# Two matrix-vector products of batch 1 on TensorE instead of VectorE, in a decode layer with its gradients

## The chip, the core and the metric

The kernel runs on one core of a Trainium2 chip. The core has a matrix engine (TensorE, PE in the profile), three engines for elementwise work (VectorE or DVE, ScalarE or ACT, GpSimd or POOL), a queue engine (SyncE or SP), 16 DMA engines, an on-chip memory SBUF of 128 partitions and an accumulator memory PSUM of eight banks. The metric is the device time of one execution in microseconds. Differences of about one per cent are at the edge of what can be told apart here.

## The reference

The layer is one decode step of attention over a cache, followed by a two-layer perceptron with ReLU, both with a layer norm ahead and a residual. Wanted are the output and the gradients with respect to seven of the inputs:

```python
h  = x + attention(layernorm(x), k_cache, v_cache, wq) @ wo
h2 = h + relu(layernorm(h) @ w1) @ w2
_out, _vjp = jax.vjp(_f, A_x, A_k_cache, A_v_cache, A_wq, A_wo, B_w1, B_w2)
```

(The first two lines are the reference's in short.) There are B = 2 batches with one token each, D = 640, H = 32 heads of 128, a cache of 4096 positions per head, and a hidden width Dff = 1728. Everything is bf16. K and V caches are 64 tiles of 1 MB each, and their gradients (out_2, out_3) are as large, so nearly all of the 363 MB moved are cache tiles.

Two small products of the backward pass are the subject here, both a weight matrix times a gradient vector of one batch:

- gx2 = w1 x ghf: 640 results, each a sum over 1728 (ghf is the gradient at the hidden layer, masked by ReLU);
- go = wo x gh1: 32 heads x 128 results, each a sum over 640 (gh1 is the gradient at h).

## The kernel before

The work is a list of *turns*, written out by hand as generators that are stepped against each other. The first sweep (`p1_iter`) visits the 64 pairs of batch and head: it loads K and V (1 MB each), transposes K in groups of blocks on TensorE (L405; ACT copies the result from PSUM, L410), forms scores, softmax and the products with V. The second sweep (`p2_iter`) visits the pairs again. In each of its turns TensorE transposes V in four groups of four f32 blocks (L426, copied by ACT at L431), takes products with go (L439) into `dp`, VectorE forms `gsp` (L823) and the two gradients gK and gV in halves of 128 x 2048 elements (L810), and POOL's queue stores them (L848, L867). V is loaded once more for it (tile `Wt`, L447, SP's queue), except for a few heads whose tile was kept. The two sweeps overlap for a while; from about 510 us on the second runs alone.

Between them lies the perceptron of each batch, `middle_gen`, a background generator. Its steps are dealt out by credit: at every step of the sweep `bg_step` adds a rate (0.8 in the part that matters here) and runs background steps until their own prices, the numbers they yield, have used it up. For batch 1 it runs beside turns 13 and following of the second sweep.

There the two products are made on VectorE. The gradient vector lies in columns, so `bcast_cols` (L619) spreads it first to a row on all partitions: TensorE multiplies broadcast columns by the identity into PSUM, and ACT copies the row to SBUF (tiles `fbc` and `hbc`). Then `ttr` (L640) multiplies a stretch of the natural weight tile with the row and sums along it: for w1 15 calls of 576 elements (five chunks of D, three thirds of Dff), for wo 32 calls of 640 elements, one a head. Each call waits for a `turn()` (L647): the main loop hands out one such slot in three of a turn's steps (L1154).

When a group of heads is summed, the rest of `go_group` (L665 to L686) rounds it, makes the paired form `gom` that the second sweep needs, and the products with MT that give the query's gradient `GQc`; it then marks the heads as done. The groups of batch 1 are heads 27 to 31, then eight at a time from 0.

What follows depends on it. After the mark ("w1", 1) the w1 tile is given up and `fin_gen` starts: the outer products of the weight gradients (`outer_rows`, L895), which use the PSUM banks of the list "o" in rotation, are copied to SBUF by ACT (L923), or one in three by VectorE (L921) once all heads are done, and stored from ACT's queue. After the last head `gx_gen` starts: it transposes wq on TensorE (L981), with ACT copying (L983), and takes products (L991), one group behind the transposes. `mlp_out` follows the heads in `middle_gen`. The transposes of all of these share two PSUM banks (role "tps") and five SBUF buffers (tag XT).

Of the kernel before, what the change touches and what calls it, by code (L numbers as in the profile page):

```python
# [7 lines left out]
FP32 = mybir.dt.float32  # L8
# [7 lines left out]
def kernel(  # L16
# [638 lines left out]

    def go_group(b, h0, h1, hbc):

        hs = slice(h0, h1)
        n = h1 - h0
        go32 = small.tile([128, GH], FP32, tag="go32", bufs=1, name="go32")  # L660
        for k in range(n):
            yield from turn()
            ttr(wo_t[:, h0 + k, :], hbc[:], go32[:, k:k + 1], D)
            yield 0.9
        nc.vector.tensor_copy(out=goc[:, hs, b], in_=go32[:, 0:n])  # L665
        pr = small.tile([128, GH], FP32, tag="pr", bufs=1, name="pr")
        nc.vector.tensor_tensor(out=pr[:, 0:n], in0=goc[:, hs, b], in1=OU[:, b, hs], op=ALU.mult)
        yield from wait(2)
        pair_rows(gom, goc, hs, slice(b, b + 1))
        yield from wait(2)  # L670
        d_ps = pst([128, 2, GH], FP32, "mid", "d_ps")
        nc.tensor.matmul(d_ps[:, 0, 0:n], lhsT=ones_f32, rhs=pr[:, 0:n], start=True, stop=True)
        for k in range(n):
            h = h0 + k
            nc.tensor.matmul(d_ps[:, 1, k:k + 1], lhsT=MTs.pop((b, h))[:], rhs=goc[:, h, b:b + 1],
                             start=True, stop=True)
        nc.vector.tensor_scalar(out=negdot[:, hs, b], in0=d_ps[:, 0, 0:n], scalar1=-1.0, scalar2=None, op0=ALU.mult)
        ud = small.tile([128, GH], FP32, tag="ud", bufs=1, name="ud")
        nc.vector.tensor_tensor(out=ud[:, 0:n], in0=Uc[:, b, hs], in1=negdot[:, hs, b], op=ALU.mult)
        mg = small.tile([128, GH], FP32, tag="mg", bufs=1, name="mg")  # L680
        nc.vector.tensor_tensor(out=mg[:, 0:n], in0=d_ps[:, 1, 0:n], in1=rt[:, b, hs], op=ALU.mult)
        nc.vector.tensor_tensor(out=ud[:, 0:n], in0=mg[:, 0:n], in1=ud[:, 0:n], op=ALU.add)
        nc.vector.tensor_scalar(out=GQc[:, hs, b], in0=ud[:, 0:n], scalar1=SCALE, scalar2=None, op0=ALU.mult)
        for h in range(h0, h1):
            done.add(("go", b, h))
        yield  # L686

    def mlp_out():

        ml32 = small.tile([128, ND, B], FP32, tag="ml32", bufs=1, name="ml32")  # L690
        nc.vector.memset(ml32[:], 0.0)
        for k in range(NW2):
            while free["q"] < 1:
                yield
            t = load_w2(k, "q", "(p c) d -> p c d")
            yield from wait(12)
            c1 = min(NF, (k + 1) * FP)
            m_ps = pst([128, ND, B], FP32, "mid", "mlp_ps")
            for c in range(ND):
                for cf in range(k * FP, c1):  # L700
                    kc = f_kc(cf)
                    nc.tensor.matmul(m_ps[:, c, :], lhsT=t[0:kc, cf - k * FP, c * 128:(c + 1) * 128],
                                     rhs=arow[0:kc, cf, :], start=(cf == k * FP), stop=(cf == c1 - 1))
            give(t)
            yield
            nc.vector.tensor_tensor(out=ml32[:], in0=m_ps[:], in1=ml32[:], op=ALU.add)
        ml_bf = small.tile([128, ND, B], BF16, tag="ml_bf", bufs=1, name="ml_bf")
        nc.vector.tensor_copy(out=ml_bf[:], in_=ml32[:])
        y_bf = small.tile([128, B, ND], BF16, tag="y_bf", bufs=1, name="y_bf")
        nc.vector.tensor_tensor(out=y_bf[:].rearrange("p b c -> p c b"), in0=h1c[:], in1=ml_bf[:], op=ALU.add)  # L710
        yield from wait(3)
        for b in range(B):
            store_row(y_bf[:, b, :], ND, out_0[b].rearrange("s (c p) -> (s c) p", p=128))
            yield

    def middle_gen(b):
        while a_next[0] < (b + 1) * H // OG:
            if o_next[0] < (b + 1) * H // OG:
                o_group()
                yield  # L720
                yield
            a_group()
            yield
        at_bf = small.tile([128, ND], BF16, tag="at_bf", bufs=1, name="at_bf")
        nc.vector.tensor_copy(out=at_bf[:], in_=asum[:, b, :])
        nc.vector.tensor_tensor(out=h1c[:, :, b], in0=xg32[:, b, :], in1=at_bf[:], op=ALU.add)
        h32 = small.tile([128, 1, ND], FP32, tag="h32", bufs=1, name="h32")
        nc.vector.tensor_copy(out=h32[:, 0, :], in_=h1c[:, :, b])
        yield ("a", b)
        u_out(b)  # L730
        yield from ln_fwd(h32[:], 1, x2c[:, :, b:b + 1], rstd2[:, b:b + 1])
        hf_ps = pst([128, NF], FP32, "mid", "hf_ps")
        for cf in range(NF):
            kc = f_kc(cf)
            for c in range(ND):
                nc.tensor.matmul(hf_ps[0:kc, cf:cf + 1], lhsT=w1_t[:, c, cf * 128:cf * 128 + kc],
                                 rhs=x2c[:, c, b:b + 1], start=(c == 0), stop=(c == ND - 1))
            yield 0.25
        nc.vector.tensor_scalar(out=acol[:, 0:NFF, b], in0=hf_ps[:, 0:NFF], scalar1=0.0, scalar2=None, op0=ALU.max)
        if F_rem:  # L740
            nc.vector.tensor_scalar(out=acol[0:F_rem, NFF, b:b + 1], in0=hf_ps[0:F_rem, NFF:NF],
                                    scalar1=0.0, scalar2=None, op0=ALU.max)
        if b == B - 1:
            ar_ps = pst([128, NFF, B], FP32, "mid", "ar_ps")
            for cf in range(NFF):
                for c in range(ND):
                    nc.tensor.matmul(ar_ps[:, cf, :], lhsT=w1_t[:, c, bass.ds(cf, 128, step=NFF)],
                                     rhs=x2c[:, c, :], start=(c == 0), stop=(c == ND - 1))
                yield 0.25
            nc.vector.tensor_scalar(out=arow[:, 0:NFF, :], in0=ar_ps[:], scalar1=0.0, scalar2=None, op0=ALU.max)  # L750
            if F_rem:
                nc.vector.tensor_copy(out=arow[:, NFF, :], in_=acol[:, NFF, :])
        mask = small.tile([128, NF], FP32, tag="mask", bufs=1, name="mask")
        nc.vector.tensor_single_scalar(out=mask[:], in_=acol[:, :, b], scalar=0.0, op=ALU.is_gt)
        nc.vector.tensor_tensor(out=ghfc[:, :, b], in0=ga[:, b, :], in1=mask[:], op=ALU.mult)
        yield from wait(3)
        fbc = cols.tile([128, Dff], BF16, tag="fbc", name="fbc")
        gx2 = small.tile([128, 1, ND], FP32, tag="gx2", bufs=1, name="gx2")
        gx2p = small.tile([128, ND, 3], FP32, tag="gx2p", bufs=1, name="gx2p")
        FW = Dff // 3  # L760
        spread_f = bcast_cols(one(ghfc, b), NF, f_kc, fbc)
        have = 0
        for k in range(3):
            while have < min(Dff, (k + 1) * FW):
                next(spread_f)
                have += 512
                yield
            for c in range(ND):
                yield from turn()
                ttr(w1_t[:, c, k * FW:(k + 1) * FW], fbc[:, k * FW:(k + 1) * FW], gx2p[:, c, k:k + 1], FW)  # L770
                yield 0.85
        nc.vector.reduce_sum(out=gx2[:, 0, :], in_=gx2p[:], axis=AX.X)
        yield ("w1", b)
        yield from ln_bwd(gx2[:], x2c[:, :, b:b + 1], rstd2[:, b:b + 1], gc[:, :, b:b + 1], gh1c[:, :, b:b + 1], 1)
        hbc = cols.tile([128, D], BF16, tag="rowbc", name="hbc")
        yield from bcast_cols(one(gh1c, b), ND, lambda c: 128, hbc)
        yield ("gh1", b)

        first = H - KEPT[b]
        bounds = [(first, first + 2), (first + 2, H)] if b == 0 else [(first, H)]  # L780
        bounds += [(h, min(first, h + GH)) for h in range(0, first, GH)]
        for h0, h1 in bounds:
            yield from go_group(b, h0, h1, hbc)
        if b > 0:
            yield from mlp_out()

# [166 lines left out]
    def gx_gen(fin):  # L953
# [11 lines left out]
        for c in range(ND):  # L965
# [1 line left out]
                fetch()  # L967
                yield 0.0
            if acc is None:
                banks["o"].remove(6)  # L970
                acc = ps.tile([128, ND, B], FP32, tag="bank6", bufs=1, name="gx_ps")
            t = tiles[c][0]
            todo = list(range(H))
# [139 lines left out]
    for n, (i, j) in enumerate(plan):  # L1113
# [15 lines left out]
        if i is None and ("w1", 1) in done and fin is None:  # L1129
# [1 line left out]
            fin = tc.alloc_tile_pool(name="fin", bufs=1)  # L1131
            big2 = tc.alloc_tile_pool(name="big2", bufs=1)
            more_home("f", big2)
            banks.update(sps=[2, 3], o=[4, 5, 6])
            bg2.append(("fin", fin_gen(fin)))
            bg3.append(("gx", gx_gen(fin)))
        late[0] = all(("go", B - 1, h) in done for h in range(H))
# [82 lines left out]
```

## Time and profile before

| | us |
|---|---|
| median of three runs | 943.43 (940.11 to 949.95) |
| the profiled execution | 942.44 |
| its span | 940.6 |

| engine | busy us | share of the span |
|---|---|---|
| PE (products) | 761.7 | 81% |
| PE (weight loads, beside the products) | 636.0 | 68% |
| DVE | 664.2 | 71% |
| ACT | 550.4 | 59% |
| POOL | 143.1 | 15% |

DMA moved 363.02 MB, a mean of 386 GB/s over the span. A busy PE in this profile is not PE at its peak, since matmuls are pipelined and their ends are modelled. The row PEclk gives the clock that TensorE was granted, in tenths of full speed. In a row of a group the columns are: source line, engine, operation, what is written from what, shapes and count; busy us and the mean of one in ns; the idle time of the engine just before them and what ended it. In a row of waits: the engine and line that waited, the one that released it, total us, times, longest.

### The profile page before, as it was taken

How to read it: one execution, taken by the hardware profiler on the slowest of the kernel's cores; microseconds unless marked ns; L12 is line 12 of the kernel's file. 1: busy time of each engine (PE TensorE's matmuls, PEld its weight loads, DVE VectorE, ACT ScalarE, POOL GpSimd, SP SyncE). 2: the span in 40 equal slices, each digit the busy share in tenths (PEclk: the TensorE clock that was granted, in tenths of full speed). 3: DMA queues.
4: the chain of work that ended last, by engine and by line, in shares of the span. 5: the costliest groups of instructions: out<-in, count | busy, mean ns of one | idle time of the engine just before them, and what ended most of it. 6: DMA issues, size and time to landing. Idle time of an engine off the chain costs nothing.

```text
span 940.6 us, 26794 instructions
## 1 busy us (share of the span) xinstructions
PE 761.7 (81%) x11482; PEld 636.0 (68%) x11482; DVE 664.2 (71%) x1256; ACT 550.4 (59%) x1162; POOL 143.1 (15%) x249
## 2 busy tenths in 40 slices
PE   5999898998997888797977837767878887888883
PEld 5888787887877777786867726556656665575652
DVE  4555677866776878777778879778797455465675
ACT  3667566667775767676733626535655564565652
POOL 1222111121000101001011112111121111010111
PEclk9999999999999999899896866655655555565656
DMA  9999999997778999999999999999999999999998
GB/s 348 419 400 409 408 388 410 413 418 284 273 290 326 362 391 423 422 408 423 396 359 375 406 425 382 394 378 403 405 395 392 424 426 423 341 393 388 338 421 360
DMA packets 59478, 363.02 MB, mean 386 GB/s; under 512 B 5696, under 2 KB 15552, under 8 KB 19168
## 3 DMA queue, kind: packets, MB, share of 16 engines
q1 hardware_dynamic: 37920, 212.18, 57.6%
q0 software_dynamic: 18432, 134.23, 34.5%
q10 hardware_dynamic: 3008, 14.91, 4.0%
q8 instruction: 90, 1.47, 0.6%
q14 instruction: 28, 0.23, 0.1%
HBM read 212.16 MB, written 149.13 MB: 384 GB/s over the span
## 4 chain that ended last, share of the span: by engine, by line
PE 39%; DMA 26%; DVE 17%; ACT 11%; issue 6%; POOL 0%; SPq 0%; POOLq 0%; ACTq 0%; DVEq 0%
DMA Kt<-in_A_k_cache_dram 10%; PE t_ps L426 9%; DMA out_dram<-gV 8%; PE m_ps L460 7%; PE t_ps L405 6%; DMA out_dram<-gK 6%; ACT t_sb L410 5%; DVE gV L810 4%; PE s_ps L416 4%; DVE gK L810 3%; PE o_ps L914 3%; DVE pk L467 3%; ACT t_sb L431 2%; PE u_ps L485 2%; DVE junk L642 2%
## 5 line engine op out<-in xcount | busy, mean ns | idle before, releaser
L410 ACT COPY t_sb<-t_ps 128x1024 bf16<-128x1024 bf16 x223 | 216.5, 1012 | 46.4 <-PE t_ps L405 41.5
L431 ACT COPY t_sb<-t_ps 128x512 f32<-128x512 f32 x256 | 149.9, 588 | 153.2 <-PE t_ps L426 150.2
L426 PE MATMUL t_ps<-ident_f,Wt 128*128 128x128 f32 x848 | 192.6, 374 | 4.3 <-ACT t_sb L410 1.7
L460 PE MATMUL m_ps<-pk,Vt 128*128 128x129 bf16 x2048 | 192.2, 223 | 1.0 <-DVE pk L467 0.6
L467 DVE TENSOR_TENSOR pk<-Kt,ep 128x2048 bf16<-128x2048 bf16 x128 | 156.3, 1221 | 34.0 <-ACT ep L510 33.9
L810 DVE TENSOR_TENSOR gV<-rb,pp 128x2048 bf16<-128x2048 bf16 x128 | 152.8, 1219 | 28.6 <-DMA out_dram<-gV 20.8
L810 DVE TENSOR_TENSOR gK<-rb,gsp 128x2048 bf16<-128x2048 bf16 x128 | 152.4, 1225 | 28.1 <-DMA out_dram<-gK 16.6
L405 PE MATMUL t_ps<-ident_bf,Kt 128*128 128x128 bf16 x2048 | 154.5, 227 | 15.6 <-DMA Kt<-in_A_k_cache_dram 15.5
L426 PEld LDWEIGHTS t_ps<-ident_f,Wt 128*128 128x128 f32 x848 | 133.2, 193 | 33.0 <-issue 21.6
L460 PEld LDWEIGHTS <-Vt 128*128 128x128 bf16 x2048 | 129.0, 99 | 29.2 <-issue 29.2
L405 PEld LDWEIGHTS <-Kt 128*128 128x128 bf16 x2048 | 127.6, 101 | 17.6 <-DMA Kt<-in_A_k_cache_dram 17.4
L439 PEld LDWEIGHTS <-t_sb 128*128 128x128 bf16 x2048 | 95.3, 106 | 40.2 <-ACT t_sb L431 18.4
L416 PE MATMUL s_ps<-qc,t_sb 128*128 128x1 bf16 x2048 | 88.9, 164 | 20.3 <-ACT t_sb L410 19.0
L439 PE MATMUL dp_ps<-gom,t_sb 128*128 128x2 bf16 x2048 | 94.9, 167 | 8.9 <-ACT t_sb L431 8.0
L416 PEld LDWEIGHTS <-t_sb 128*128 128x128 bf16 x2048 | 75.1, 97 | 33.0 <-ACT t_sb L410 29.8
L867 POOL DMA_DIRECT2D out_dram<-gV x64 | 34.3, 536 | 293.4 <-DVE gV L810 232.0
L556 POOL COPY P_bf<-ep 128x32 bf16<-128x32 bf16 x40 | 43.7, 1092 | 220.6 <-ACT ep L510 220.6
L848 POOL DMA_DIRECT2D out_dram<-gK x64 | 34.1, 533 | 274.4 <-DVE gK L810 220.5
L923 ACT CAST ot<-o_ps 128x512 bf16<-128x512 f32 (+4 forms) x134 | 60.1, 478 | 19.9 <-PE o_ps L914 14.4
L551 DVE TENSOR_REDUCE rmax<-s_ps 128x1 bf16<-128x32 f32 x64 | 12.3, 192 | 61.2 <-PE s_ps L416 61.2
L837 ACT ACTIVATE rb<-dp_ps,rt 128x256 bf16<-128x256 f32 x64 | 30.5, 477 | 40.9 <-PE dp_ps L832 40.2
L642 DVE CUSTOM_DVE_ANT_0 junk<-wo_t,hbc 128x640 bf16<-128x640 bf16 x64 | 52.4, 819 | 0.2
(194 smaller groups left out, 804.3 us busy)
## 6 DMA issues: line engine op xcount, KB each, us to landing
Kt<-in_A_k_cache_dram SPq DMA_DIRECT2D x64, 1024.0 KB, 14.6
Vt<-in_A_v_cache_dram SPq DMA_DIRECT2D x64, 1024.0 KB, 11.3
out_dram<-gV POOLq DMA_DIRECT2D x64, 1024.0 KB, 11.1
out_dram<-gK POOLq DMA_DIRECT2D x64, 1024.0 KB, 10.2
Wt<-in_A_v_cache_dram SPq DMA_DIRECT2D x53, 1024.0 KB, 10.6
wo_t<-in_A_wo_dram SPq DMA_DIRECT2D x4, 1280.0 KB, 13.0
wqs<-in_A_wq_dram SPq DMA_DIRECT2D x5, 1024.0 KB
wq_t<-in_A_wq_dram SPq DMA_DIRECT2D x5, 960.0 KB, 15.1
```

What stands on the lines that cost most here:

```text
L405: nc.tensor.transpose(t_ps[:, j, :], nat[:, g * GT + j, :], ident_bf[:])
L410: nc.scalar.copy(out=t_sb[:], in_=t_ps[:])
L416: nc.tensor.matmul(dst[:, sc:sc + 1], lhsT=t_sb[:, j, :], rhs=vec, start=True, stop=True)
L426: nc.tensor.transpose(t_ps[:, j, :], natf[:, 2 * cc:2 * cc + 2, :].rearrange("p c k -> p (c k)"), ident_f[:])
L431: nc.scalar.copy(out=t_sb[:], in_=t_ps[:])
L439: nc.tensor.matmul(dst[:, sc:sc + 2], lhsT=v[:, j, :, par], rhs=vecs[:, par, :], start=(par == 0), stop=(par == 1))
L460: nc.tensor.matmul(r["m"][:, 0:129], lhsT=r["V"][:, sc, :], rhs=r["pk"][sc // HALF][:, sc % HALF, 0:129], start=(sc == 0), stop=(sc == NSC ...
L467: nc.vector.tensor_tensor(out=p["pk"][k][:, :, 0:128].rearrange("p s (a two) -> p s a two", two=2), in0=p["K"][:, sl, :].rearrange("p s (a ...
L556: (nc.gpsimd if i < P2_AT else nc.vector).tensor_copy(out=P_bf[:, bhp, :], in_=ep[:, :, 0])
L642: nc.vector.tensor_tensor_reduce(out=junk[0:kc, 0:width], in0=in0, in1=in1, scale=1.0, scalar=0.0, op0=ALU.mult, op1=ALU.add, accum_out=acc)
L810: nc.vector.tensor_tensor(out=pairs_view(dst[:, sl, :]), in0=row.rearrange("p (a two) -> p a two", two=2)[:, None, :, :].to_broadcast([128 ...
L923: nc.scalar.copy(out=ot[0:P, k, n0:n0 + nn], in_=o_ps[0:P, 0:nn])
```

## The change

For batch 1 alone, both products go to TensorE. `turned` takes up to eight weight blocks of 128 x 128: it transposes them into one PSUM bank, ACT copies them to SBUF (a block with fewer rows by itself), and each transposed block is then multiplied by a column of the gradient into one column of an accumulator in PSUM bank 6, which had no other use at that time. There are 70 blocks of w1 in ten groups and 160 of wo in 32 groups, one a head. No row is spread any more, and `turn()` isn't asked for; the steps have prices of 0.12 a block and 0.3. The second half of `go_group` becomes `go_done`, which now reads the accumulator. Batch 0 keeps the sums on VectorE. The list "o" has two banks from its start, where before it had three until `gx_gen` took bank 6.

```diff
+    def turned(parts):
+
+        t_ps = pst([128, GT, 128], BF16, "tps", "t_ps")
+        for x, (src, kc, *_) in enumerate(parts):
+            nc.tensor.transpose(t_ps[0:kc, x, :], src, ident_bf[:])
+        t_sb = mats.tile([128, GT, 128], BF16, tag="XT", bufs=5, name="t_sb")
+        whole = sum(kc == 128 for _, kc, *_ in parts)
+        nc.scalar.copy(out=t_sb[:, 0:whole, :], in_=t_ps[:, 0:whole, :])
+        for x, (_, kc, *_) in enumerate(parts):
+            if kc < 128:
+                nc.scalar.copy(out=t_sb[0:kc, x, :], in_=t_ps[0:kc, x, :])
+        yield 0.12 * len(parts)
+        for x, (_, kc, dst, vec, first, last) in enumerate(parts):
+            nc.tensor.matmul(dst, lhsT=t_sb[0:kc, x, :], rhs=vec, start=first, stop=last)
+        yield 0.3
+
+    def go_turned(b, h0, h1):
+
+        acc = ps.tile([128, GH], FP32, tag="bank6", bufs=1, name="go_ps")
+        for h in range(h0, h1):
+            yield from turned([(wo_t[:, h, c * 128:(c + 1) * 128], 128, acc[:, h - h0:h - h0 + 1],
+                                gh1c[:, c, b:b + 1], c == 0, c == ND - 1) for c in range(ND)])
+        yield from go_done(b, h0, h1, acc)
+
+    def gx2_turned(b, gx2):
+
+        acc = ps.tile([128, ND], FP32, tag="bank6", bufs=1, name="gx2_ps")
+        for c in range(ND):
+            for f0 in range(0, NF, GT):
+                yield from turned([(w1_t[:, c, cf * 128:cf * 128 + f_kc(cf)], f_kc(cf), acc[:, c:c + 1],
+                                    ghfc[0:f_kc(cf), cf, b:b + 1], cf == 0, cf == NF - 1)
+                                   for cf in range(f0, min(NF, f0 + GT))])
+        nc.vector.tensor_copy(out=gx2, in_=acc[:])
...
+        if b == B - 1:
+            yield from gx2_turned(b, gx2[:, 0, :])
+        else:
+            yield from gx2_rows(b, gx2)
         yield ("w1", b)
...
-        hbc = cols.tile([128, D], BF16, tag="rowbc", name="hbc")
-        yield from bcast_cols(one(gh1c, b), ND, lambda c: 128, hbc)
+        if b < B - 1:
+            hbc = cols.tile([128, D], BF16, tag="rowbc", name="hbc")
+            yield from bcast_cols(one(gh1c, b), ND, lambda c: 128, hbc)
...
-            yield from go_group(b, h0, h1, hbc)
+            yield from (go_group(b, h0, h1, hbc) if b < B - 1 else go_turned(b, h0, h1))
...
-                banks["o"].remove(6)
                 acc = ps.tile([128, ND, B], FP32, tag="bank6", bufs=1, name="gx_ps")
...
-            banks.update(sps=[2, 3], o=[4, 5, 6])
+            banks.update(sps=[2, 3], o=[4, 5])
```

More of the change, by code (lines that the diff above doesn't have):

```diff
@@ L656, in go_group @@
     def go_group(b, h0, h1, hbc):
-        hs = slice(h0, h1)
-        n = h1 - h0
         go32 = small.tile([128, GH], FP32, tag="go32", bufs=1, name="go32")
-        for k in range(n):
+        for k in range(h1 - h0):
             yield from turn()
@@ L664, in go_group, with go_done @@
             yield 0.9
+        yield from go_done(b, h0, h1, go32)
+    def go_done(b, h0, h1, go32):
+        hs = slice(h0, h1)
+        n = h1 - h0
         nc.vector.tensor_copy(out=goc[:, hs, b], in_=go32[:, 0:n])
@@ L714, in mlp_out, with gx2_rows @@
             yield
+    def gx2_rows(b, gx2):
+        fbc = cols.tile([128, Dff], BF16, tag="fbc", name="fbc")
+        gx2p = small.tile([128, ND, 3], FP32, tag="gx2p", bufs=1, name="gx2p")
+        FW = Dff // 3
+        spread_f = bcast_cols(one(ghfc, b), NF, f_kc, fbc)
+        have = 0
+        for k in range(3):
+            while have < min(Dff, (k + 1) * FW):
+                next(spread_f)
+                have += 512
+                yield
+            for c in range(ND):
+                yield from turn()
+                ttr(w1_t[:, c, k * FW:(k + 1) * FW], fbc[:, k * FW:(k + 1) * FW], gx2p[:, c, k:k + 1], FW)
+                yield 0.85
+        nc.vector.reduce_sum(out=gx2[:, 0, :], in_=gx2p[:], axis=AX.X)
     def middle_gen(b):
@@ L756, in middle_gen @@
         yield from wait(3)
-        fbc = cols.tile([128, Dff], BF16, tag="fbc", name="fbc")
         gx2 = small.tile([128, 1, ND], FP32, tag="gx2", bufs=1, name="gx2")
[L759 to L772, printed above, removed]
+        if b == B - 1:
+            yield from gx2_turned(b, gx2[:, 0, :])
+        else:
+            yield from gx2_rows(b, gx2)
         yield ("w1", b)
         yield from ln_bwd(gx2[:], x2c[:, :, b:b + 1], rstd2[:, b:b + 1], gc[:, :, b:b + 1], gh1c[:, :, b:b + 1], 1)
-        hbc = cols.tile([128, D], BF16, tag="rowbc", name="hbc")
-        yield from bcast_cols(one(gh1c, b), ND, lambda c: 128, hbc)
+        if b < B - 1:
+            hbc = cols.tile([128, D], BF16, tag="rowbc", name="hbc")
+            yield from bcast_cols(one(gh1c, b), ND, lambda c: 128, hbc)
         yield ("gh1", b)
```

## The prediction

> **What bounds the kernel now.** I read the page's slices first, then 20 us windows of the second half, then the groups and the waits of the stretch in which batch 1's sums run. The lines of the slices (40 equal slices of 23.5 us):
>
> ```profile
> PE   5999898998997888797977837767878887888883
> ...
> DVE  4555677866776878777778879778797455465675
> ...
> PEclk9999999999999999899896866655655555565656
> ...
> GB/s 348 419 400 409 408 388 410 413 418 284 273 290 326 362 391 423 422 408 423 396 359 375 406 425 382 394 378 403 405 395 392 424 426 423 341 393 388 338 421 360
> ```
>
> The row to trust is GB/s: 363.02 MB have to move, and the best slices stand at 423 to 426. From 330 us on the DMA engines are never idle for long, so time can only be won where the rate is below that. The change starts near 520 us. The windows there (columns: stretch and length; busy us and count of PE, weight load, DVE, ACT, POOL; granted clock, DMA share, GB/s):
>
> ```profile
> 560.00:580.00 20.00, 11.06 (x117) 10.18 (x118) 19.59 (x38) 7.72 (x18) 4.89 (x9) 0.54 0.97 385
> 580.00:600.00 20.00, 17.20 (x183) 12.94 (x181) 17.66 (x33) 13.41 (x32) 3.40 (x8) 0.74 1.01 413
> ...
> 620.00:640.00 20.00, 16.59 (x153) 13.81 (x153) 18.86 (x36) 9.28 (x19) 4.21 (x7) 0.50 0.93 355
> ...
> 680.00:700.00 20.00, 14.23 (x123) 10.61 (x123) 19.65 (x37) 9.71 (x20) 5.37 (x10) 0.50 0.95 394
> ...
> 740.00:760.00 20.00, 16.65 (x169) 12.90 (x169) 9.80 (x12) 9.10 (x18) 2.62 (x6) 0.50 1.01 425
> ```
>
> Where VectorE is full (19.59, 18.86, 19.65 of 20 us) the rate sags; once the sums are over (740 us) VectorE is half idle and the rate is 425. The ten windows from 520 to 720 average 396 GB/s (402, 425, 385, 413, 390, 355, 410, 406, 394, 381), the four from 720 to 800 average 424.5. Loss: 200 x (1 - 396/424.5) = 13.4 us. **That is all that relief of VectorE can bring here.** The groups of 500 to 720 us:
>
> ```profile
> L426 PE MATMUL t_ps<-ident_f,Wt 128*128 128x128 f32 x361 | 80.7, 370 | 1.4 <-DMA Wt<-in_A_v_cache_dram 1.4
> ...
> L431 ACT COPY t_sb<-t_ps 128x512 f32<-128x512 f32 x110 | 64.0, 587 | 63.6 <-PE t_ps L426 61.6 <-ACT ot L923 0.9
> ...
> L642 DVE CUSTOM_DVE_ANT_0 junk<-wo_t,hbc 128x640 bf16<-128x640 bf16 x32 | 26.2, 819 | 0.2
> ...
> L642 DVE CUSTOM_DVE_ANT_0 junk<-w_t,fbc 128x576 bf16<-128x576 bf16 x15 | 11.3, 754 | 1.3 <-ACT fbc L629 1.0
> ```
>
> A turn of the second sweep (one head) needs on VectorE four halves of L810 at 1.22 us, gsp 0.28, and up to three sums at 0.82 + 0.08: 7.9 us; without sums 5.2. Its transfers, one 1 MB load and two 1 MB stores (3.15 MB), need 7.4 us at 426 GB/s. So VectorE bounds by a little, and DMA is right behind.
>
> **What the Trainium skill says.** "TensorE: Matmul & The Clock Gate", section "Wait — 56ns, not 53.3ns?": 128-column products start every 107 ns cold, 56 warm, and never under about 25 ns however narrow. The trace agrees: spacing 107 and 56 ns for bf16 transposes, 213 and 109 for f32, 25 to 27 for one- or two-column products. Same page, Part 1: activity releases the throttle; but Part 4 says that transposes do not engage the full clock. The trace leans to Part 4: up to 480 us, with real products among the transposes, the clock is near 1.0; from 700 to 800 us PE is 82% busy, mostly transposes, at 0.53. So I don't expect the added transposes to raise the clock much. "ScalarE: Activation LUTs", section "What ACT_TABLE_LOAD costs", prices a copy at 186 + 0.833 ns a column; the trace's 587 (512 columns) and 1012 ns (1024) give the same slope and a little less fixed cost.
>
> **The change part by part.** Turns are counted by the gV stores in POOL's timeline (turn 17 at 525.9 us, 21 at 560.5, 30 at 633.0, 42 at 724.6); which turn a step falls into, before and after, is read from the build's order.
>
> Removed: 32 x 0.90 + 15 x 0.84 = 41.4 us of VectorE, six row-spreading copies on ACT (3.0 us) and their 19 products. All are cover for nothing else.
>
> Added: 42 groups (10 of w1, 32 heads of wo), each a burst of transposes, an ACT copy, a burst of one-column products: 230 blocks in all. On PE a block is 107 + 27 ns at half clock, 56 + 25 at full: 31 or 19 us. On ACT: 5 x 1.01 + 5 x (0.69 + 0.27) + 32 x 0.69 = 32 us, beside some 100 of 200 us busy; ACT stays under its limit.
>
> The wait: in the build's order 22 of the 42 groups have their products directly behind their own transposes, and PE runs in order. What that handover costs is seen with the wq blocks, late in the trace:
>
> ```profile
> 810.65 1.03 PE L981 MATMUL t_ps<-ident_bf,wqs 128*128 128x128 bf16 x8
> ...
> 811.77 1.01 ACT L983 COPY t_sb<-t_ps 128x1024 bf16<-128x1024 bf16 x1 [1.37 <-PE t_ps L981]
> ```
>
> ACT starts 0.1 us after the last transpose and the next reader would start 0.1 us after the copy: 0.69 + 0.2 = 0.9 us of PE idle for a wo head, about 1.2 for a w1 group, if ACT is free. Behind it stand the turn's own transposes, its dp sums (for which gsp and gK on VectorE wait, and then POOL's store), and outer products. Bounds: 0 where other work already fills it, 1.9 where ACT has a copy in hand. I take 0.9.
>
> *w1, turns 17 to 20.* PE issue at half clock from the order: 27.6 us, at full 16.2; half the time at full (as before there) 20, plus six direct waits of 1.2 and 3 us of the turns' own: 31. The turns took 34.6 us, with 425 GB/s in 540 to 560: DMA covers it. Cost 0, gain 0.
>
> *wo, turns 21 to 29* (the sums ran on to turn 41 before: at three a turn they were paced by VectorE's slots; now by 0.8 of credit a step, up to six heads a turn). PE at half clock: nine turns at 4.5 (16 x 213 + 32 x 27 + two of 107 ns) = 40.5; 32 heads x 0.67 = 21.4; 30 outer products and 15 row products 9.7: 71.8 us; all at full clock 41.7. With a quarter of the time at full (windows: 0.54, 0.74, 0.65, 0.50): 61. Direct waits 16 x 0.9 = 14; the turns' own waits and outer products on two PSUM banks in place of three, 10 (late in the trace, with two, PE waits 22 us for 78 of them). Sum 85, against 72.5 before: **+12.5**. PE takes VectorE's place here.
>
> *Turns 30 to 41*: 91.6 us before, 36.2 MB, 85 us at full rate. Without sums VectorE needs 5.2 and PE 5.9 a turn at half clock, both under DMA's 7. Loads run one or two tiles ahead while PE is the bound; at half that, 2 us less: 83. **-8.5.**
>
> *From turn 42*: the work is the same, mlp_out, wq blocks and outer products come one to three turns earlier. On SP's queue w2 and wq loads move ahead of up to three Wt loads, 1 MB each that would be needed soon after anyway; on POOL nothing moves. Cost 0, bounds -5 to +5: the sags there (337 GB/s at 800, 318 at 860) come of PE and ACT waiting for each other over outer products and will be dealt out anew. PSUM bank 6 was idle: the accumulator costs nothing itself.
>
> Sum: +12.5 - 8.5 = +4 on a profiled time of 942.4 (span 940.6): 946.4. The median of the runs is 943.4, 1 us more: **947**.
>
> **The rivals.** *VectorE's relief comes through.* If ACT's copies fall into time in which PE would wait for DMA anyway, or PE's denser work holds the clock up (at full, wo needs 42 + 14 + 10 = 66 us, just DMA's 66 for 28.2 MB), all 13.4 us are won: 930. For it: VectorE at 98% just where the rate sags, PE busy 68% of 560 to 640. Against: the 22 direct waits, and heads come five or six to a turn, so a turn swings between 5 and 13 us while buffers hold two or three tiles.
>
> *PE and ACT in lockstep: slower.* Place: turns 21 to 29. With the clock at half throughout and outer products on two banks, I step through turn 23 (six heads, eight outer products) to 15 us and turn 25 to 11; nine turns give 98: +25, less 8.5: 959. It decides from a wait of some 1.5 us a group, or a clock under 0.55. For it: turns of this kind exist, late, at 14 to 17 us, with DMA nearly dry. This wait shows it:
>
> ```profile
> PE o_ps L914 <- ACT ot L923: 27.8, 31, 3.1
> ```
>
> Against: those turns also carry 24 wq transposes, and a third of the outer copies move to VectorE earlier.
>
> That the change does nothing is the likeliest case's near neighbour: one bound for another at the same price, 943.
>
> **How the numbers follow.** Trade, 0.45 (own range 938 to 954); relief, 0.27 (925 to 934); lockstep, 0.23 (953 to 966); late stage alone, 0.05, either sign. The range that leaves out two in ten: 929 to 961. One per cent, about what this measurement can tell from no change, is 934 to 953: faster 0.28, the same 0.40, slower 0.32.
>
> **What would show it.** Right: VectorE under 14 of 20 us from 560 on, no L642 there; a group of go_ps products waiting for ACT's t_sb copy by some 0.9 us, about twenty times; turns 21 to 29 about 85 us; rate near 424 in turns 30 to 41. Wrong: a clock near 1.0 from 560 to 640 (relief), or DMA dips there to 300 GB/s and turns of 15 us (lockstep).

## The result and the profile after

The changed kernel is **slower by 3.8%**: 980.12 us (979.14 to 985.25) against 946.54 us for the kernel before, a ratio of 1.0376 with a 95% interval of 1.0313 to 1.0439. The prediction had 947 us, a range of 929 to 961, and three directions nearly balanced. The profiled execution took 985.25 us, with a span of 983.5, so the two profiles that are compared below lie 42.9 us apart, more than the medians. In the later batches of runs the kernel before took 942 to 944 us, so the 946.54 here is a little high.

The slices of the page after, in the order of those shown of before:

```profile
PE   6999889999988897887878787777877787898882
...
DVE  4556777766958778677685653455676546564765
...
PEclk9999999999999999999856555565556556565756
DMA  9999999996888999999799785878999999998998
GB/s 354 419 400 409 398 401 407 416 389 237 293 317 332 349 421 423 423 419 423 287 395 383 279 346 194 324 298 326 398 421 379 409 380 389 392 407 353 391 422 369
```

A slice is 24.6 us here. In the 23rd to 28th (541 to 688 us) VectorE has the room that the change was to give it: 6, 5, 3, 4, 5, 5 tenths where it had 7 to 9. But the rate there is only 279, 346, 194, 324, 298 and 326 GB/s, and the DMA row, never under 9 tenths there before, shows 7, 8, 5, 8, 7, 8. The row of before:

```profile
DMA  9999999997778999999999999999999999999998
```

The 20 us windows after (same columns as in the prediction; the last three numbers are granted clock, DMA share and GB/s):

```profile
540.00:560.00 20.00, 15.26 (x169) 13.31 (x166) 10.18 (x21) 10.08 (x19) 2.81 (x4) 0.57 0.70 251
560.00:580.00 20.00, 15.23 (x166) 13.47 (x167) 12.21 (x18) 11.84 (x26) 3.09 (x6) 0.50 0.94 378
580.00:600.00 20.00, 15.36 (x140) 11.42 (x139) 5.66 (x10) 10.60 (x21) 2.08 (x5) 0.50 0.78 279
600.00:620.00 20.00, 15.78 (x176) 13.38 (x175) 11.43 (x21) 10.63 (x22) 3.21 (x6) 0.56 0.61 213
...
640.00:660.00 20.00, 16.04 (x207) 13.69 (x206) 9.93 (x17) 11.88 (x21) 2.56 (x5) 0.62 0.74 281
```

No engine is full, and still little moves: PE is busy 15 to 16 of 20 us, ACT 10 to 12, VectorE 6 to 12, and in four of these five windows DMA stands idle for a fifth to two fifths of the time. That is the picture of engines waiting for each other. Over 520 to 720 us the DMA share averages 0.84, where before it was 0.99: 200 x 0.15, some 30 us of idle transfer time, most of what lies between these two profiles.

What waits for what, from the waits of the stretch from 500 us on (who waited, for whom, us in total, times, longest):

```profile
POOL out_dram L894 <- DVE gK L856: 214.7, 44, 15.7
...
DVE gsp L869 <- PE dp_ps L439: 70.8, 32, 13.6
PE o_ps L960 <- ACT ot L969: 37.1, 48, 2.0
...
ACT t_sb L699 <- PE t_ps L696: 26.9, 34, 1.7
...
PEld L705 <- ACT t_sb L699: 25.4, 26, 1.6
```

The last row is the new wait: 26 times, among 42 groups of products, PE waits for the copy of the group's own blocks, 0.98 us each. The row above it says that ACT stood waiting for the transposes 34 times, so mostly it was ready to copy at once. The first two rows lie in the same turns: gsp waits for the last dp sums of a turn up to 13.6 us, and the store of gK up to 15.7 us. How much of them comes of the new wait, the first experiment tells. The same two rows before:

```profile
POOL out_dram L848 <- DVE gK L810: 170.7, 47, 7.2
...
DVE gsp L823 <- PE dp_ps L439: 32.2, 18, 4.7
```

Two pieces of the timeline, from the same heavy turn (turn 23):

```profile
592.50 0.69 PE L696 MATMUL t_ps<-ident_bf,wo_t 128*128 128x128 bf16 x5
...
593.28 0.69 ACT L699 COPY t_sb<-t_ps 128x640 bf16<-128x640 bf16 x1 [0.16 <-PE t_ps L696]
...
594.03 0.21 PEld L705 LDWEIGHTS <-t_sb 128*128 128x128 bf16 x5 [1.10 <-ACT t_sb L699]
...
601.63 0.69 ACT L699 COPY t_sb<-t_ps 128x640 bf16<-128x640 bf16 x1 [1.50 <-PE t_ps L696]
602.22 0.26 ACT L969 CAST ot<-o_ps 96x128 bf16<-96x128 f32 x1
602.53 0.26 PE L960 MATMUL o_ps<-gr,ar 2*96 2x128 bf16 x1 [1.00 <-ACT ot L969]
602.73 0.38 PE L439 MATMUL dp_ps<-gom,t_sb 128*128 128x2 bf16 x8
...
603.14 0.28 DVE L869 SCALAR_TENSOR_TENSOR gsp<-dp_ps,negdot,P_bf 128x64 bf16<-128x64 f32 x1 [13.56 <-PE dp_ps L439]
...
606.39 0.53 POOL L894 DMA_DIRECT2D out_dram<-gK  x1 [15.74 <-DVE gK L856]
```

In the first three lines PE transposes, ACT copies, and PE's products wait 1.10 us for the copy. Later in the turn PE's stops end at an outer product instead (602.53, 1.00 us): it needs one of two banks, which ACT empties at 602.22, behind the copy of a head's blocks. Over turns 21 to 29 the two kinds of stop weigh the same in PE's rows: 11.6 us, 15 times, before products of these blocks, and 12.2 us, 14 times, before outer products. (The row above of 25.4 us is that of the weight loads, PEld, which come ahead of the products; 15.7 us of it fall into these turns.) The eight dp sums at 602.73 had their input from ACT since 596.75; they stand in PE's order behind three heads and three outer products. gsp has waited 13.56 us for them, and so has POOL with the store.

Stages by turns (counted by gV stores in POOL's timeline, us, and MB landed in them):

| turns | before | after | products one group later (first experiment) |
|---|---|---|---|
| 17 to 20 (w1) | 34.6, 14.3 MB | 37.0, 11.3 MB | 28.3, 11.2 MB |
| 21 to 29 (wo) | 72.5, 28.2 MB | 109.2, 31.6 MB | 94.5, 31.6 MB |
| 30 to 41 | 91.6, 36.2 MB | 97.9, 38.7 MB | 96.7, 38.7 MB |
| 42 to 61 | 199.1, 78.8 MB | 193.6, 76.1 MB | 193.3, 76.0 MB |

Most of the loss lies in the wo turns, +36.7 us. Some transfers are moved from one stage to another: w1's turns carry 3 MB less than before, so that their +2.4 us hides a part of the loss. The DMA share shows it: 0.84 over w1's turns and 0.76 over wo's, where it was 1.01 and 0.98. That is 6 and 26 us of idle transfer time. Turn 17 itself began 3.9 us later in this execution (at 529.8 us, against 525.9). The first new transposes start only at 528.7 us, so most of this delay isn't theirs.

### The profile page after: what moved, and what is told of

Same layout as the page of the kernel before. It is cut to its first block, busy times and chain, and to the rows that moved or that the text cites. A ratio compares the mean times of both kernels' runs of the same rounds, so it can differ in the third digit from the quotient of the medians.

```text
span 983.5 us, 27657 instructions
## 1 busy us (share of the span) xinstructions
PE 808.0 (82%) x11923; PEld 676.5 (69%) x11923; DVE 632.7 (64%) x1167; ACT 575.2 (58%) x1198; POOL 141.9 (14%) x249
## 3 DMA queue, kind: packets, MB, share of 16 engines
q1 hardware_dynamic: 37920, 212.18, 55.9%
q0 software_dynamic: 18432, 134.23, 33.0%
## 4 chain that ended last, share of the span: by engine, by line
PE 50%; DMA 18%; ACT 15%; DVE 10%; issue 5%; POOL 0%; ACTq 0%; POOLq 0%; SPq 0%; DVEq 0%
PE t_ps L426 14%; DMA Kt<-in_A_k_cache_dram 13%; PE m_ps L460 7%; PE t_ps L405 6%; PE o_ps L960 5%; ACT t_sb L410 4%; DMA out_dram<-gV 3%; ACT t_sb L431 3%; PE s_ps L416 3%; PE dp_ps L439 3%; DVE gV L856 2%; PE t_ps L696 2%; DVE pk L467 2%; ACT t_sb L699 2%; ACT ot L969 2%
## 5 line engine op out<-in xcount | busy, mean ns | idle before, releaser
L426 PE MATMUL t_ps<-ident_f,Wt 128*128 128x128 f32 x848 | 201.7, 387 | 4.9 <-ACT t_sb L1028 2.5
L405 PE MATMUL t_ps<-ident_bf,Kt 128*128 128x128 bf16 x2048 | 157.5, 229 | 21.4 <-DMA Kt<-in_A_k_cache_dram 21.1
L426 PEld LDWEIGHTS t_ps<-ident_f,Wt 128*128 128x128 f32 x848 | 139.9, 201 | 36.8 <-issue 20.3
L405 PEld LDWEIGHTS <-Kt 128*128 128x128 bf16 x2048 | 130.1, 103 | 23.8 <-DMA Kt<-in_A_k_cache_dram 23.6
L439 PEld LDWEIGHTS <-t_sb 128*128 128x128 bf16 x2048 | 97.7, 108 | 32.8 <-ACT t_sb L431 15.9
L416 PEld LDWEIGHTS <-t_sb 128*128 128x128 bf16 x2048 | 75.7, 97 | 32.0 <-ACT t_sb L410 28.6
L869 DVE SCALAR_TENSOR_TENSOR gsp<-dp_ps,negdot,P_bf 128x64 bf16<-128x64 f32 x64 | 18.0, 281 | 72.4 <-PE dp_ps L439 71.4
L969 ACT CAST ot<-o_ps 128x512 bf16<-128x512 f32 (+3 forms) x129 | 57.5, 473 | 6.2 <-PE o_ps L960 4.9
L572 ACT CAST MT<-m_ps 128x128 bf16<-128x128 f32 x64 | 17.0, 266 | 58.5 <-PE m_ps L460 58.5
## 6 DMA issues: line engine op xcount, KB each, us to landing
Vt<-in_A_v_cache_dram SPq DMA_DIRECT2D x64, 1024.0 KB, 13.4
```

The costliest lines, as they stand in the source:

```text
L405: nc.tensor.transpose(t_ps[:, j, :], nat[:, g * GT + j, :], ident_bf[:])
L416: nc.tensor.matmul(dst[:, sc:sc + 1], lhsT=t_sb[:, j, :], rhs=vec, start=True, stop=True)
L426: nc.tensor.transpose(t_ps[:, j, :], natf[:, 2 * cc:2 * cc + 2, :].rearrange("p c k -> p (c k)"), ident_f[:])
L439: nc.tensor.matmul(dst[:, sc:sc + 2], lhsT=v[:, j, :, par], rhs=vecs[:, par, :], start=(par == 0), stop=(par == 1))
L969: nc.scalar.copy(out=ot[0:P, k, n0:n0 + nn], in_=o_ps[0:P, 0:nn])
```

## The experiments

Theories: **A**, the handover: products directly behind their own transposes stop PE for the length of ACT's copy. **B**, load: 230 blocks are too much for PE at its clock, wherever they stand. **C**, bursts: up to six heads a turn hold up that turn's dp sums, and the buffers don't bridge it. **D**, the third bank of the outer products is missed. Beside these, what relief of VectorE is worth at all. Each ratio is to runs of the kernel before in the same batch of runs (its medians there: 942 to 944 us).

### Products one group later

The transposes of the next group are issued before the products of the last, as `gx_gen` does it.

```diff
-        yield 0.12 * len(parts)
-        for x, (_, kc, dst, vec, first, last) in enumerate(parts):
-            nc.tensor.matmul(dst, lhsT=t_sb[0:kc, x, :], rhs=vec, start=first, stop=last)
-        yield 0.3
+            nxt = (t_sb, parts)
+            yield 0.12 * len(parts)
+        if prev is not None:
+            for x, (_, kc, dst, vec, first, last) in enumerate(prev[1]):
+                nc.tensor.matmul(dst, lhsT=prev[0][0:kc, x, :], rhs=vec, start=first, stop=last)
+            yield 0.3
+        prev = nxt
```

> The changed kernel, with the products of each group issued one group later, behind the next group's transposes; the work is the same. Theory A (the handover from transposes to copy to products is what costs): most direct waits go, 22 x 0.8 us at least, and stores come earlier with them: 955 to 965 us. Theory B (TensorE has too much to issue at half clock, wherever the products stand): within 5 us of the changed kernel, 975 to 985. Theory C (bursts of up to six heads hold up each turn's last dp sums): 970 to 980.

Measured: 953.29 us, ratio 1.0112 (1.0083 to 1.0140). Of 3.76% slower, 1.12% are left: about 25 us are won by the order alone, with the same work on every engine. The group of products in 500 to 720 us:

```profile
L711 PEld LDWEIGHTS <-t_sb 128*128 128x128 bf16 x230 | 11.1, 106 | 4.9 <-ACT t_sb L703 2.3 <-issue 2.1
```

The wait for the copy went from 25.4 us to 2.3, by 23 us: nearly as much as the time. It agrees by stages too, where as many MB landed as in the changed kernel: w1's turns are 8.7 us shorter, with this wait down from 9.7 us to 1.2, and wo's turns 14.7 us, with the wait down from 15.7 to 1.1. PE's waits before outer products in wo's turns stayed (12.2, then 12.6 us). So theory A holds: this wait lay on the path nearly whole. B falls as the main cause, since PE has the same work.

C is not settled by it. Turn 23, with its six heads, took 22.1 us in the changed kernel and still takes 20.5, and the row of gsp is little shorter than the 70.8 us there:

```profile
DVE gsp L875 <- PE dp_ps L439: 60.3, 33, 12.0
```

So most of gsp's waiting, and of the store's behind it (195.5 us where it was 214.7), does not come of the handover.

### Two banks for the outer products, on the kernel before

```diff
-                banks["o"].remove(6)
-            banks.update(sps=[2, 3], o=[4, 5, 6])
+            banks.update(sps=[2, 3], o=[4, 5])
```

> The kernel before, with the one part of the change that touches the outer products: the list o has two PSUM banks from its start in place of three; the sums stay on VectorE. Theory D (the third bank is what is missed): slower by 10 us or more. Theories A, B and C: no more than 4 us slower, 943 to 950.

Measured: 947.90 us, ratio 1.0066 (1.0046 to 1.0086), 6 us. That is more than the 4 us that A, B and C allowed, though within the 943 to 950 us put beside it, and less than D. The row of the outer products' bank, to be set beside 27.8 us and 31 times of the kernel before:

```profile
PE o_ps L914 <- ACT ot L923: 45.9, 47, 5.9
```

### No sums of batch 1 on VectorE, on the kernel before

```diff
-                ttr(w1_t[:, c, k * FW:(k + 1) * FW], fbc[:, k * FW:(k + 1) * FW], gx2p[:, c, k:k + 1], FW)
+                if b == 0:
+                    ttr(w1_t[:, c, k * FW:(k + 1) * FW], fbc[:, k * FW:(k + 1) * FW], gx2p[:, c, k:k + 1], FW)
...
-            ttr(wo_t[:, h0 + k, :], hbc[:], go32[:, k:k + 1], D)
+            if b == 0:
+                ttr(wo_t[:, h0 + k, :], hbc[:], go32[:, k:k + 1], D)
```

> The kernel before, with batch 1's 47 VectorE sums left out (their results are filled in from other data); rows are still spread, steps keep their places. It bounds what relief of VectorE can bring. By the prediction's sum of lost DMA rate: 13 us faster than before, 928 to 936. If VectorE was not a bound at all in that stretch: within 4 us of before.

Measured: 940.59 us, ratio 0.9978 (0.9956 to 1.0000): 2 us, at most 4, not 13. The whole stretch from 520 to 720 us in one window, of this run,

```profile
520.00:720.00 200.00, 146.74 (x1527) 120.34 (x1527) 134.61 (x206) 106.50 (x233) 37.30 (x75) 0.62 1.00 399
```

of the kernel before,

```profile
520.00:720.00 200.00, 142.73 (x1461) 115.40 (x1460) 169.46 (x294) 104.24 (x226) 36.46 (x75) 0.63 0.99 396
```

and of the changed kernel:

```profile
520.00:720.00 200.00, 157.45 (x1638) 128.86 (x1637) 106.54 (x172) 108.04 (x214) 28.11 (x59) 0.56 0.84 320
```

35 us less of VectorE bring 3 GB/s: the DMA share was 0.99 already and went to 1.00. By this column the DMA engines are full at 396 to 399 GB/s here, and not only at 425. The chain of work that ended last says the same of the kernel before: over 520 to 720 us 44% of it are stores (of gK, gV and ot), and 3.3% VectorE's sums. So, with the steps in their places, the gain that the change was after is 2 us.

### Copies on VectorE

The changed kernel with `nc.vector.tensor_copy` in place of `nc.scalar.copy` for the transposed blocks.

> The changed kernel, with the copies of the transposed blocks on VectorE, which has room now, in place of ACT. Theory A in the form that ACT's queue delays the copy: 960 to 972 us. If the wait is the copy's own length: within 5 us of the changed kernel, or slower where a copy stands behind a 1.2 us half of a gradient.

Measured: 975.72 us, ratio 1.0337 (1.0270 to 1.0405). The interval overlaps that of the changed kernel, so nothing is shown to be won. The wait stays as long, on the other engine:

```profile
PEld L705 <- DVE t_sb L699: 27.8, 28, 3.5
```

So ACT's queue was not what held the copies up; ACT had mostly been ready for them. That the copy's length is what counts isn't shown either: on VectorE a copy takes 0.51 us in the mean, on ACT 0.73, and the waits are no shorter. Single waits are longer (3.5 us); the expectation named the reason, a copy behind halves of a gradient.

### Fewer heads a turn

```diff
-        yield 0.12 * len(parts)
+        yield 0.3 * len(parts)
...
-        yield 0.3
+        yield 0.5
```

> The changed kernel with higher prices of its steps (0.3 a block and 0.5 for the products in place of 0.12 and 0.3): at most two or three heads fall into a turn, each with its direct wait as before; the wo stage reaches over some ten more turns. Theory C (bursts hold up each turn's last dp sums, and buffers can't bridge turns of 15 to 20 us): 955 to 965 us. Theory A alone (each handover costs its 0.8 us wherever it stands): within 8 us of the changed kernel, 972 to 988.

Measured: 962.14 us, ratio 1.0199 (1.0152 to 1.0246). Half of the loss goes, some 17 us. But the handover is not as before, which the expectation took for granted: with the higher prices other work comes to stand between a group's transposes and its products, and most of the wait for the copy goes too. Its row, to be set beside 25.4 us, 26 times:

```profile
PEld L705 <- ACT t_sb L699: 5.9, 12, 1.0
```

That is 19.5 us less of the wait, and at the same time no turn from 21 to 29 is longer than 13.9 us. The run takes away waits and bursts together, so it can't tell A from C. Turns 21 to 29 take 77 us (28.7 MB) where the changed kernel took 109.2, and the DMA share is 0.95 to 1.01 up to 620 us. What is left comes later: 0.81 at 620 and 0.61 at 700 us.

### The last dp sums earlier

On the kernel before, and on the changed kernel with products one group later, the eight dp sums of a turn's last group are issued at the end of that turn:

```diff
-            pair_matvec(p["dp"], p.pop("T3"), 3, gom[:, hp, bp, :, :])
...
         outer_half(gV, c["rb"][:, 0:128], c["pp"], 0)
         yield
+        pair_matvec(c["dp"], c.pop("T3"), 3, go)
```

> The kernel before, with the last eight dp sums of a turn issued at the end of that turn in place of the beginning of the next, so that no background step stands between them and gsp. If late dp sums were costing something before: 3 to 8 us faster. If DMA bounds it all anyway: within 3 us of before, 939 to 945.

Measured: 938.84 us, ratio 0.9956 (0.9936 to 0.9977), 4 us faster than the kernel before: the one version here that beats both. Its row of gsp, to be set beside 32.2 us, 18 times, at most 4.7:

```profile
DVE gsp L822 <- PE dp_ps L439: 9.8, 8, 2.1
```

> The changed kernel with the products one group later and the early dp sums of the run before. If the rest of the loss (953 against 942) is stores that come late behind background work: 943 to 948. If it is TensorE's load or the two banks: 950 to 955.

Measured: 954.47 us, ratio 1.0106 (1.0065 to 1.0147): no gain over the later products alone, though the row of gsp is less than half of the 60.3 us there:

```profile
DVE gsp L874 <- PE dp_ps L439: 28.8, 17, 6.6
```

Late dp sums are not what is left of the loss there.

### Later products and the third bank

The accumulators move to bank 7, and VectorE copies each group's result out; the list o is as in the kernel before.

```diff
-        acc = ps.tile([128, GH], FP32, tag="bank6", bufs=1, name="go_ps")
+                acc = pst([128, 16], FP32, "mid", "go_ps")
...
+                nc.vector.tensor_copy(out=put(g - 1), in_=acc[:, 0:1])
...
-            banks.update(sps=[2, 3], o=[4, 5])
+            banks.update(sps=[2, 3], o=[4, 5, 6])
```

> The changed kernel with the products one group later, and the accumulators in the shared bank 7, copied out by VectorE after each group, so that the outer products keep their third bank. The two-bank run on the kernel before cost 6 us; if that adds up: 945 to 949. If banks don't matter once TensorE is loaded: 951 to 955.

Measured: 950.71 us, ratio 1.0083 (1.0043 to 1.0122), between the two expectations. It overlaps the run without the third bank (1.0083 to 1.0140), so the bank's share, 6 us on the kernel before, isn't resolved here. The run also adds copies on VectorE, which wait 19.5 us for PE's products of wo, so it is not the bank alone that differs.

### Both cures

Later products and the higher prices, 0.3 a block and 0.5.

> The changed kernel with both cures at once: products one group later, and the higher prices that allow two or three heads a turn. If waits and bursts are two causes that add up, nearly all of the loss is gone: 942 to 948. If they are one cause seen twice: 950 to 956, as with the later products alone.

Measured: 957.94 us, ratio 1.0167 (1.0146 to 1.0189): neither; worse than later products alone. The windows at its weak place:

```profile
680.00:700.00 20.00, 16.73 (x148) 12.21 (x148) 13.35 (x14) 11.04 (x21) 3.83 (x9) 0.50 0.92 378
700.00:720.00 20.00, 15.41 (x137) 11.34 (x134) 9.61 (x15) 11.86 (x26) 1.94 (x5) 0.50 0.60 243
```

The last product of a head starts at 731.5 us here and at 643.7 with the low prices, so heads now fall among outer products that came after them with the low prices. The higher prices alone have their weak place there too (0.61 at 700 us). That this collision is the cause is argued from the order, not shown by a run of its own.

### Without the products

The changed kernel with the 230 products left out and the accumulators filled by VectorE.

> The changed kernel with the 230 products left out (the accumulators are filled by VectorE): transposes and copies stay where they are, and nothing on TensorE waits for a copy of them; prices and bursts as in the changed kernel. Theory A: like the run with later products, less 6 us of issue, 944 to 954. If transposes and bursts are to blame: 965 or more.

Measured: 951.52 us, ratio 1.0105 (1.0080 to 1.0129). As with the later products (1.0112), by another way: transposes, copies, bursts and two banks together cost 10 us, and the products with their waits cost the rest. The run takes away more than the waits, namely the products' issue, some 6 us, and VectorE's waits for their results (15.2 us, 3 times, in the changed kernel). The run with later products keeps both and comes to the same time, so neither can be the main part.

### Everything together

Later products, higher prices, third bank, early dp sums.

> Later products, higher prices, third bank for the outer products and early dp sums together. The kernel before with early dp sums alone measured 939 against 944. If TensorE's blocks can be hidden wholly: 936 to 941, level with that; if their issue at half clock still costs: 942 to 948.

Measured: 941.81 us, ratio 1.0001 (0.9979 to 1.0024). The blocks can be hidden so far that the kernel is level with the one before; but that one with early dp sums alone is faster. Which of the four parts makes this run so much better than the two cures together wasn't separated. PE's waits before outer products fell from 44.5 us, 56 times, with the two cures to 18.0 us, 23 times, which points to the third bank, but the early dp sums differ as well.

### The w1 half alone

`gx2_turned` as in the change, wo on VectorE, three banks.

```diff
-            yield from (go_group(b, h0, h1, hbc) if b < B - 1 else go_turned(b, h0, h1))
+            yield from go_group(b, h0, h1, hbc)
```

> The w1 half of the change alone: the ten groups of w1 on TensorE as in the changed kernel, wo's 32 sums on VectorE and three banks for the outer products as before. The prediction's step (DMA covers it, cost 0): within 4 us of before. If a direct wait costs the same there as in the wo stage (six of 22): 948 to 954.

Measured: 946.63 us, ratio 1.0044 (1.0020 to 1.0068): 4 us slower (2 to 6) for ten groups, with a DMA share of 0.82 over turns 17 to 20. So w1's part is not free either.

## Why the prediction was wrong

Two terms of its sum failed. Turns 21 to 29 were put at +12.5 us and took +36.7; turns 30 to 41 were put at -8.5 us and took +6.3. The second rests on the bound that comes first here.

**"All that relief of VectorE can bring": 13.4 us.** This step failed. It read lost time from GB/s, against the best rate elsewhere. The column beside it, DMA share, stood at 0.97 to 1.01 in most of the same windows (0.93 and 0.95 in two): by that column 200 us held 1.8 us of idle DMA. The run without the sums measured 2 us. Nor did the rate follow VectorE: 600 to 620 us, a window that is in the average but not among the lines shown, had VectorE busy 13.17 of 20 us and 390 GB/s. VectorE's 19.6 of 20 us was true and beside the point: without the sums VectorE is still busy 18.78 us from 560 to 580 us. With this bound falls the ground of the rival "relief" (0.27 of the chances).

**Turns 30 to 41: -8.5 us.** Failed for the same reason: 97.9 us were measured in place of 83. These turns were priced at 426 GB/s; 38.7 MB went at 396, with the DMA share at 0.99 to 1.01 from 680 to 780 us. Without sums on VectorE at all (on the kernel before) they took 93.3 us, so there was nothing to give back.

**Turns 21 to 29: +12.5 us.** The mechanism was named rightly, products behind their own transposes with PE in order, and its unit was near: 0.98 us a wait measured against 0.9. The size was off: 109.2 us against 85. Two terms of that sum were too small. PE's issue time was put at 61 us with a quarter of the time at full clock. The granted clock over these turns was 0.55, about a tenth of the time at full; the counts in the trace at the spacings that the prediction gives make 68 us, an estimate. The stops of all kinds were put at 24 us; what is left of 109.2 beside 68 is 41. The waits for the copies were near their 14 us (15.7), but the stops before outer products alone took 12.2 us, where 10 were to cover these and the turns' own. The other 13 us are smaller stops that weren't gone into. So this step failed above all in the time in which PE does not issue, 41 us in place of 24. That the waits for the copies lay on the path, the first experiment shows, 23 us of wait and 25 us of time.

How the stops become the kernel's time is seen in part. Over 560 to 680 us the chain of work that ended last runs through PE and ACT, with ACT's copies of these blocks 11.7% of it (14 us), while DMA stands partly idle. A way to the stores would be the dp sums that gsp, gK and POOL's store need, which come last in PE's order. But with the products one group later, issuing these sums earlier won nothing, and on the changed kernel itself it wasn't tried, so this way isn't shown.

**w1: cost 0.** DMA did not cover these turns (the share is 0.70 in 540 to 560). The run with w1 alone on TensorE costs 4 us; in the changed kernel the first experiment wins 8.7 us in these turns. The prediction counted six direct waits there; 11 were measured, two of them of wo's first heads.

**The two banks** were counted within 10 us of waits; alone, on the kernel before, they cost 6 us.

**The rival "lockstep"** had the place, the mechanism and nearly the price of the wo stage (98 us for nine turns, 109 measured). Its total, 959, was too low by the 8.5 us that were to come back and by 11 in the stage itself, and its chance, 0.23, was too low. It was to decide from a wait of some 1.5 us a group or a clock under 0.55; the wait was 0.98 us and the clock 0.55, so it came nearest without its condition being clearly met. The signs that were set for it appeared: DMA down to 213 GB/s between 560 and 640 us, turns of 13 to 22 us. What argued against it, that the late heavy turns also carry wq transposes, carried no weight: those transposes are one group ahead of their products, and these were not.

**The clock.** The Trainium skill's "TensorE: Matmul & The Clock Gate" says in Part 4 that transposes don't engage the full clock. The traces fit that: PE is busier from 520 to 720 us than before (157 against 143 us) and its clock is lower (0.56 against 0.63). No run isolates it; with the same blocks and the products one group later PE is busy 167 us at a clock of 0.60.

The rest adds up: of the 3.76%, 2.64 (about 25 us) are the handover; the remaining 1.12 (about 10 us) are what the kernel without products loses too, with two banks (6 us alone), w1 (4 us alone, waits included) and the load of the transposes, which overlap and weren't separated further.

## What to carry to other kernels

Before an engine is relieved, ask whether the one behind it has any room. Here the DMA share told it, and the rate didn't. If you can, leave the work out and measure: that bounds the gain for the price of one run. On an engine that works in order, don't put a consumer directly behind a producer whose result goes through another engine; one group of distance took about 25 of 34 us here with the same work. And look at what stands last in a turn's order: on the kernel before, moving eight small products forward brought 4 us, and taking 35 us off VectorE about 2. On the changed kernel with later products the same move brought nothing, so it has to be measured each time. Last, read the waits of an experiment too: higher prices were to leave the handover alone, and took most of its wait away.

## What the runs showed that I had not expected

By its busy share, DMA can be full at quite different rates: in the kernel before, a share of 0.99 at 396 GB/s from 520 to 720 us (1.00 at 399 without the sums), and of 1.01 at 425 from 740 to 760. The page's queues differ too: loads on q1 moved 212.18 MB in 57.6% of 940.6 us, which is 392 GB/s while its packets ran, and POOL's stores on q0 134.23 MB in 34.5%, 414 GB/s. What sets the difference wasn't tried.
